# Product two of the last half of a down projection as a joint inner product, in a kernel that is bound by TensorE

## The chip, the cores and the metric

The kernel runs on one core of a Trainium2 chip. The metric is the device time of one execution in microseconds (us), taken as the median of several executions.

PE is TensorE's matmuls, PEld its weight loads, DVE is VectorE, ACT is ScalarE, SP (SyncE) the queue that issues most transfers. PSUM is the memory that matmuls write (this kernel declares eight banks of 512 float32 columns per partition), SBUF the working memory.

## The reference, cut to what matters

```python
# x: (1, 2048, 1024), bf16
xn = _layernorm(x, axis=-1)
s = _A_ref(xn, A_wqkv, A_wo)                       # linear attention
g = _silu(_B_ref(xn, B_w_gate, B_w_up, B_w_down))  # (silu(xn@wg) * (xn@wu)) @ wd
return x + s * g
```

The change concerns the last product, h @ wd. There h has 3584 columns, wd is 3584 x 1024.

## The kernel before

Large products are made with Winograd's form of Strassen's scheme: a product of 2 x 2 blocks takes seven block products rather than eight, at the price of sums of weight blocks and x blocks. "Product 2" (step 2 below) is one of those seven. The kernel cuts its token rows into two halves, `p`, and the output columns of the down projection into two halves, `h`. "The last half" is `(p, h) == (1, 1)`. In each half two sets (`w` = 0, 1) of 256 output columns, each two blocks of 128, run side by side.

For products 1 and 5 the two sets are joined: together they form a 2 x 2 block product again, and the scheme is applied a second time. That is the class `Joint`: seven inner products of 256 columns, in four parts a to d.

```python
class Set:
    def put1(self, a):                 # product 1 is in bank a: copy it to a second bank b
        self.a = a
        self.b = balloc()
        act([bank_r[a]], [bank_r[self.b]], ps[self.b][:, :], ps[a][:, :], ACT.Identity)
    def step(self, m):
        ...
        elif m == 2:
            self.grp(2, self.a, False)   # 14 matmuls of 512 columns, on top of product 1
            self.out(0, 0, self.a)
        elif m == 6:
            self.grp(6, self.b, False)
            self.c = balloc()
            tt(..., ps[self.c][:, :], ps[self.b][:, :], self.s5.ap(F32), ALU.add)
        ...
class Joint:
    def step(self, part):
        ...
        if part == 1:
            self.grp(6, y, 0)
            self.grp(2, x, 0)
            # the half-bank add: x's right half = y's left half + s
            tt([bank_r[y], s.r], [bank_r[x]], ps[x][:, 256:512], ps[y][:, 0:256], s.ap(F32), ALU.add)
        elif part == 2:
            self.grp(7, y, 0)            # writes y's left half: must wait for that add
            self.grp(3, x, 1)
            ...
ON_D  = "L 7_0 K0 6_1 7_1 K1 nj1a 3_0 nj1b 3_1 S nj1c 4a nj5a nj1d 4b nj5b n2_0 nj5c n2_1 nj5d n6_0"
END_D = "7_0 6_1 7_1 3_0 3_1 4_0 4_1"
```

Strings such as `END_D` are the order of steps: `n2_0` is product 2 of set 0 of the next half, `nj5b` part b of its joint product 5. A planner in the kernel then orders the instructions of every engine once, at build time, by estimated durations and deadlines. Each engine executes its list in order; only waits on semaphores remain.

## Time and profile before

| | before |
|---|---|
| median of the first 3 runs (range) | 712.78 us (711.15 to 713.37) |
| span of the profiled execution | 710.2 us |
| PE busy | 704.5 us, 4181 matmuls |
| DVE busy | 631.2 us |
| ACT busy | 424.9 us |

The span runs from the first to the last instruction on the core and is shorter than the time. Busy time counts overlapping neighbours once. The prediction below shows the lines.

### The profile page before, as it was taken

How to read it: one execution, taken by the hardware profiler on the slowest of the kernel's cores; microseconds unless marked ns; L12 is line 12 of the kernel's file. 1: busy time of each engine (PE TensorE's matmuls, PEld its weight loads, DVE VectorE, ACT ScalarE, POOL GpSimd, SP SyncE). 2: the span in 40 equal slices, each digit the busy share in tenths (PEclk: the TensorE clock that was granted, in tenths of full speed). 3: DMA queues.
4: the chain of work that ended last, by engine and by line, in shares of the span. 5: the costliest groups of instructions: out<-in, count | busy, mean ns of one | idle time of the engine just before them, and what ended most of it. 6: DMA issues, size and time to landing. Idle time of an engine off the chain costs nothing.

```text
span 710.2 us, 11444 instructions
## 1 busy us (share of the span) xinstructions
PE 704.5 (99%) x4181; PEld 388.1 (55%) x4181; DVE 631.2 (89%) x1534; ACT 424.9 (60%) x827; POOL 13.0 (2%) x34
## 2 busy tenths in 40 slices
PE   8999999999999999999999999999999999999997
PEld 3444445555555555556556455555555555565654
DVE  6999858989999999998958999999999999798863
ACT  5788766988679676664212257876886756531212
POOL 2111000000000000000000000000000000000000
PEclk9999999999999999999999999999999999999999
DMA  9654133346664253326498854322716241646763
GB/s 301 143 95 115 31 118 120 119 133 194 175 181 147 96 160 108 110 63 174 123 243 212 219 133 148 111 68 94 208 60 193 75 149 60 181 138 160 144 156 96
DMA packets 140871, 98.64 MB, mean 139 GB/s; under 512 B 34960, under 2 KB 137872, under 8 KB 140816
## 3 DMA queue, kind: packets, MB, share of 16 engines
q1 hardware_dynamic: 139472, 96.69, 49.1%
q10 hardware_dynamic: 1344, 1.25, 0.5%
q8 instruction: 32, 0.52, 0.3%
q14 instruction: 23, 0.19, 0.1%
HBM read 77.59 MB, written 12.71 MB: 127 GB/s over the span
## 4 chain that ended last, share of the span: by engine, by line
PE 98%; DMA 1%; SPq 0%; issue 0%; DVE 0%; ACT 0%
PE ps L309 98%; DMA H<-in_A_wqkv_dram 1%; PE ps L316 0%; DVE TM L453 0%; SPq L456 0%; SPq L760 0%; ACT TM L442 0%
## 5 line engine op out<-in xcount | busy, mean ns | idle before, releaser
L309 PE MATMUL ps<-X,W 128*128 128x512 f16 (+2 forms) x1348 | 282.6, 349 | 0.0
L442 ACT ACTIVATE TM<-ps 128x512 f16<-128x512 f32 (+3 forms) x386 | 202.7, 554 | 100.8 <-PE ps L309 97.3
L309 PE MATMUL ps<-H,W 128*128 128x512 f16 (+2 forms) x1096 | 218.6, 351 | 0.1
L309 PEld LDWEIGHTS ps<-X,W 128*128 128x128 f16 (+1 forms) x1348 | 130.0, 98 | 101.6 <-ACT H L442 1.0
L453 DVE TENSOR_TENSOR W<-W 128x256 f16<-128x256 f16 (+5 forms) x400 | 178.8, 479 | 2.7 <-PE ps L309 1.9
L309 PEld LDWEIGHTS ps<-H,W 128*128 128x128 f16 (+1 forms) x1096 | 105.9, 98 | 95.4 <-DVE ps L453 1.1
L453 DVE TENSOR_TENSOR ps<-ps,TM 128x256 f32<-128x256 f32 (+1 forms) x250 | 131.4, 527 | 14.8 <-PE ps L309 11.5
L442 ACT ACTIVATE ps<-ps 128x512 f32<-128x512 f32 (+1 forms) x174 | 85.7, 493 | 89.9 <-PE ps L309 89.4
L442 ACT ACTIVATE H<-ps 128x512 f16<-128x512 f32 (+1 forms) x132 | 78.5, 605 | 37.8 <-PE ps L309 37.8
L309 PE MATMUL ps<-P,W 128*128 128x256 f16 (+1 forms) x492 | 94.5, 318 | 0.0
L453 DVE TENSOR_TENSOR H<-H 128x1024 f16<-128x1024 f16 (+5 forms) x130 | 73.7, 581 | 0.7 <-ACT H L442 0.5
L442 ACT ACTIVATE TM<-TM 128x512 f16<-128x512 f32 (+1 forms) x70 | 44.0, 631 | 45.6 <-DVE TM L453 45.1
L309 PEld LDWEIGHTS ps<-P,W 128*128 128x128 f16 (+1 forms) x492 | 47.9, 98 | 27.0 <-ACT TM L442 0.8
L309 PE MATMUL ps<-W 128*128 128x256 f16 (+1 forms) x326 | 61.2, 282 | 0.0
L453 DVE TENSOR_TENSOR H<-H,TM 128x512 f16<-128x512 f16 (+1 forms) x120 | 48.0, 417 | 8.5 <-ACT H L442 8.3
L453 DVE TENSOR_TENSOR TM<-ps,TM 128x512 f32<-128x512 f32 (+3 forms) x63 | 41.6, 660 | 12.9 <-PE ps L309 12.0
L309 PEld LDWEIGHTS ps<-W 128*128 128x128 f16 (+1 forms) x326 | 31.1, 98 | 31.0 <-DVE ps L453 0.8
L309 PE MATMUL ps<-H,X 128*128 128x512 bf16 (+1 forms) x150 | 35.2, 379 | 0.4 <-DMA H<-in_A_wqkv_dram 0.4
L453 DVE TENSOR_TENSOR TM<-TM 128x512 bf16<-128x512 f16 (+2 forms) x73 | 29.2, 412 | 6.1 <-ACT TM L442 4.4
L309 PE MATMUL ps<-H,P 128*128 128x512 bf16 (+1 forms) x110 | 26.8, 379 | 0.0
L453 DVE TENSOR_TENSOR H<-ps,TM 128x512 f16<-128x512 f32 (+1 forms) x35 | 24.0, 686 | 2.2 <-PE ps L309 1.3
L453 DVE TENSOR_TENSOR TM<-TM,W 128x512 f16<-128x512 f16 (+1 forms) x39 | 14.1, 363 | 11.8 <-ACT TM L442 11.7
(111 smaller groups left out, 417.0 us busy)
## 6 DMA issues: line engine op xcount, KB each, us to landing
W<-in_B_w_up_dram SPq DMA_DIRECT2D x14, 1024.0 KB, 5.6
W<-in_B_w_gate_dram SPq DMA_DIRECT2D x13, 1024.0 KB, 5.3
W<-in_B_w_down_dram SPq DMA_DIRECT2D x14, 896.0 KB, 6.1
H<-r_scratch SPq DMA_DIRECT2D x32, 128.0 KB, 3.9
W<-m_scratch SPq DMA_DIRECT2D x4, 1024.0 KB, 5.4
s_scratch<-TM SPq DMA_DIRECT2D x32, 128.0 KB, 2.0
TM<-in_A_x_dram SPq DMA_DIRECT2D x16, 256.0 KB, 4.0
W<-in_A_x_dram SPq DMA_DIRECT2D x15, 256.0 KB, 3.4
```

Source lines behind the costliest of these rows:

```text
L309: last = h.matmul(o, l, r, start=st, stop=sp, skip_group_check=True)
L442: q = PL.op("act", reads, writes, lambda h: h.activation(o, i, func, **kw), nel(o) / (1000.0 if "bias" in kw or not isinstance(kw.get("sca ...
L453: return dve(reads, writes, lambda h: h.tensor_tensor(o, a, b, op), nel(o), 1.92 if fast else 0.96)
```

## The change

The intent: apply the second level of the scheme to product 2 as well, in the last half only. Product 1 can then no longer stay in the bank under product 2, so it is kept in SBUF and added afterwards. The x sums need space, and the R00 blocks of the hidden tensor are dead once product 1 of the last half is done. The core of the diff:

```diff
             def put1(self, a):
+                if self.two:
+                    self.b = a
+                    self.s1 = (self.s1r or s1_ring).take()
+                    act([bank_r[a]], [self.s1.r], self.s1.ap(F32), ps[a][:, :], ACT.Identity)
+                    return
+            def put2(self, x):
+                ...
+                d = (self.d2r or d2_ring).take()
+                tt([bank_r[x], self.s1.r], [d.r], d.ap(F32), ps[x][:, :], self.s1.ap(F32), ALU.add)
+                bfree(x)
+                self.evac(0, 0, d.ap(F32), d.r, None)
+        def tj_two():
+            B = {(k, j): hq("R10", k, j, 0, NU) for k in range(2) for j in range(2)}
+            t = {m: hq("R00", k, j, 0, NU) for m, (k, j) in TJ2.items()}
+            sub(t[7], B[1, 1], B[0, 1])
+            sub(t[5], B[0, 1], B[0, 0])
+            sub(t[6], B[1, 1], t[5])
+            sub(t[4], B[1, 0], t[6])
+                if (p, h) == (1, 1):
+                    self.joint["2"] = Joint(partial(self.jops, 2), lambda w, b: self.sets[w].put2(b))
+                    for s in self.sets:
+                        s.two = True
-        END_D = "7_0 6_1 7_1 3_0 3_1 4_0 4_1"
+        ON_E = "L 7_0 K0 6_1 7_1 K1 nj1a 3_0 nj1b 3_1 S nj1c 4a nj5a nj1d 4c nj5b 4d nj5c n6_0 nj5d"
+        END_D = "j2a 7_0 j2b 6_1 j2c 3_0 j2d 7_1 3_1 4_0 4_1"
```

Cut: facilities that this version leaves switched off (weight sums kept in DRAM, joint product 2 elsewhere), a cap on the planner's tuning passes, and moved buffers at the start of the second token half (the sums of one weight, the raw load of another).

More of the change, by code (lines that the diff above doesn't have):

```diff
@@ L130, in tune @@
         front = 0.0
-        while True:
+        for _ in range(90):
             prev, last, work, at = {}, {}, 0.0, None
@@ L584, in build_kernel, with __init__ @@
         class Set:
-            def __init__(self, ops, evac, dring):
-                self.ops, self.evac, self.dring, self.direct = ops, evac, dring, None
+            def __init__(self, ops, evac, dring, s1r=None, d2r=None):
+                self.ops, self.evac, self.dring, self.direct, self.two = ops, evac, dring, None, False
+                self.s1r, self.d2r = s1r, d2r
             def out(self, i, j, b):
@@ L612, in put1 @@
                 act([bank_r[a]], [bank_r[self.b]], ps[self.b][:, :], ps[a][:, :], ACT.Identity)
+            def put2(self, x):
+                if self.direct is not None:
+                    self.direct(0, 0, x, self.s1)
+                    bfree(x)
+                    return
+                d = (self.d2r or d2_ring).take()
+                tt([bank_r[x], self.s1.r], [d.r], d.ap(F32), ps[x][:, :], self.s1.ap(F32), ALU.add)
+                bfree(x)
+                self.evac(0, 0, d.ap(F32), d.r, None)
             def put5(self, e):
@@ L709, in build_kernel @@
         LINK = "7_0 nj1a 3_0 7_1 nj1b nj5a 3_1 nj1c nj5b 4_0 nj1d nj5c 4_1 n2_0 nj5d n6_0 n2_1 n6_1".split()
+        LINK3 = "7_0 nj1a 3_0 7_1 nj1b nj5a 3_1 nj1c nj5b 4_0 nj1d nj5c 4_1 nj2a nj5d n6_0 nj2b n6_1 nj2c".split()
         last_pair = [None]
@@ L722, in feed @@
             else:
-                for w in LINK:
+                for w in LINK3 if "2" in pair.joint else LINK:
                     if w[0] == "n":
@@ L727, in feed @@
                         prev.do(w)
+                    if w == "7_0" and prev is not None and prev.joint and "2" in prev.joint:
+                        prev.do("j2d")
             last_pair[0] = pair
@@ L1114, in strips, with wload @@
                     [hb(n, nm)[1].keys for n in range(8)])
-        def wload(src, joint, dt=BF16, rd=(), inh=(0, 0)):
+        w_scr = nc.dram_tensor("w_scratch", [18, 128, 4 * KB], FP16)
+        i_scr = nc.dram_tensor("i_scratch", [18, 2, 128, KB], FP16)
+        s1_ring, in2_ring, d2_ring = (Places([(a, o * KB) for a, o in at], 2 * KB) for at in (
+            [(H, 36)],
+            [(H, 36)],
+            [(H, 36)]))
+        TWO = []
+        NOSP = [('q', 1), ('g', 1), ('u', 1), ('g', 2), ('u', 2), ('g', 3), ('u', 3), ('g', 4), ('u', 4), ('g', 5), ('u', 5), ('g', 6), ('u', 6), ('q', 0), ('g', 0), ('u', 0), ('s', 0), ('s', 1)]
+        CH, IH, put = {}, {}, {}
+        def wload(src, joint, tag, dt=BF16, rd=(), inh=(0, 0)):
+            p, kind, n = tag
+            kept = {"g": 0, "u": 7, "s": 14, "q": 16}[kind] + n
             if inh[0]:
@@ L1128, in wload @@
             if inh[1]:
-                cs, keys = strips("T1", FP16)
+                cs, keys = strips((None, "T1", "T3")[inh[1]], FP16)
                 cv = cs.rearrange("p (m w) (kt n) -> p m w kt n", w=2, n=128)
                 cr = [Region(keys[2 * q] + keys[2 * q + 1]) for q in range(4)]
+                call, csem = cs, dsem("wch%d" % inh[1])
             else:
@@ L1135, in wload @@
                 cr = [c.sub(q * 2 * KB, 2 * KB).r for q in range(4)]
-            sums({(k, i): v[:, :, 4 * k:4 * k + 4, i * 128:i * 128 + 128] for k in range(2) for i in range(2)},
+                call, csem = c.ap(FP16), dsem("wc%s%d" % (c.a.name, c.off // KB))
+            cl = Region(sum((r.keys for r in cr), ()))
+            keep = (kind, n) not in NOSP
+            if p and keep:
+                kv = w_scr[kept]
+                dma([named("ws", kept)], [cl], call, kv.rearrange("p (b t) -> p b t", t=512) if inh[1] else kv, csem, 1024 * KB)
+            else:
+              sums({(k, i): v[:, :, 4 * k:4 * k + 4, i * 128:i * 128 + 128] for k in range(2) for i in range(2)},
                  [cv[:, q] for q in range(4)], [sr], cr)
+              if keep:
+                put.setdefault((kind, n), []).append((CH.get((kind, n), "j1a"), lambda: dma(
+                    [cl], [named("ws", kept)], w_scr[kept], call, dsem("wk%s%d" % (c.a.name, c.off // KB)), 1024 * KB,
+                    after=PL.lastpe)))
             def block(m):
@@ L1148, in wload @@
             inner = {}
-            for m in joint:
+            for m in joint + ((2,) if p and (kind, n) in TWO else ()):
                 bl, r = block(m)
-                t = in_ring.take()
+                t = (in2_ring if m == 2 else in_ring).take()
                 tv = t.ap(FP16).rearrange("p (m kt n) -> p m kt n", m=4, n=128)
@@ L1154, in wload @@
                 A = {(k, i): bl[:, i, 2 * k:2 * k + 2, :] for k in range(2) for i in range(2)}
-                sums(A, [tv[:, q] for q in range(4)], [r], tr)
+                place = "%s%d" % (t.a.name, t.off // KB)
+                held = named("wi", kept, m)
+                if p and m != 2 and keep:
+                    dma([held], [t.r], t.ap(FP16), i_scr[kept, m // 5], dsem("wi" + place), 256 * KB)
+                else:
+                    sums(A, [tv[:, q] for q in range(4)], [r], tr)
+                    if not p and keep:
+                        put.setdefault((kind, n), []).append((IH.get((kind, n), "j%da") % m, partial(
+                            dma, [t.r], [held], i_scr[kept, m // 5], t.ap(FP16), dsem("wj" + place), 256 * KB)))
                 inner[m] = (A, r, tv, tr)
@@ L1174, in build_kernel, with x_inner @@
         xin, qin = {}, {}
-        def x_inner(v, xin=xin, places=IN_AT):
-            for m, at in zip((1, 5), places):
+        def x_inner(v, xin=xin, places=IN_AT, ms=(1, 5)):
+            for m, at in zip(ms, places):
                 ap, r = v[XOF[m]]
@@ L1182, in x_inner, with joint_of @@
                 tt([r], [t[1][1]], t[1][0], B[1, 1], B[0, 1], ALU.subtract, True)
-                tt([r], [r], B[0, 1], B[0, 1], B[0, 0], ALU.subtract, True)
-                tt([r], [t[0][1]], t[0][0], B[1, 1], B[0, 1], ALU.subtract, True)
+                f, fr = t[3] if len(t) > 3 else (B[0, 1], r)
+                tt([r], [fr], f, B[0, 1], B[0, 0], ALU.subtract, True)
+                tt([r, fr], [t[0][1]], t[0][0], B[1, 1], f, ALU.subtract, True)
                 tt([r, t[0][1]], [t[2][1]], t[2][0], B[1, 0], t[0][0], ALU.subtract, True)
-                xin[m] = {1: (B[0, 0], r), 2: (B[1, 0], r), 3: (B[1, 1], r), 5: (B[0, 1], r), 6: t[0], 7: t[1], 4: t[2]}
-        def joint_of(jstat, s0, s1, xin=xin):
+                xin[m] = {1: (B[0, 0], r), 2: (B[1, 0], r), 3: (B[1, 1], r), 5: (f, fr), 6: t[0], 7: t[1], 4: t[2]}
+        def joint_of(jstat, s0, s1, xin=xin, two=False):
             def ops(m):
@@ L1194, in ops @@
                 return f
-            return {"1": Joint(ops(1), lambda w, b: (s0, s1)[w].put1(b)),
+            s0.two = s1.two = two
+            js = {"2": Joint(ops(2), lambda w, b: (s0, s1)[w].put2(b))} if two else {}
+            return {**js, "1": Joint(ops(1), lambda w, b: (s0, s1)[w].put1(b)),
                     "5": Joint(ops(5), lambda w, b: (s0, s1)[w].put5(b))}
@@ L1214, in q_load @@
         def q_load(p, s):
-            return wload(wqkv_v[:, :, s * 512:(s + 1) * 512], QJ[p][s])
+            return wload(wqkv_v[:, :, s * 512:(s + 1) * 512], QJ[p][s], (p, "q", s))
         def pq_tile(g, j):
@@ L1230, in q_pair @@
             s0, s1 = (xset(stat, w, XV[p], evac(w), d_ring) for w in range(2))
-            pair = Pair(s0, s1, joint_of(jstat, s0, s1) if QJ[p][s] else None, at)
+            pair = Pair(s0, s1, joint_of(jstat, s0, s1, two=p == 1 and ("q", s) in TWO) if QJ[p][s] else None, at)
             if go:
@@ L1287, in hb2, with gu_load @@
             return v, Region(hb(n, nm)[1].keys + hb(n + 1, nm)[1].keys)
-        def gu_load(k, n):
-            return wload((wg_v if k == "g" else wu_v)[:, :, n * 512:(n + 1) * 512], (1, 5), inh=(1, 1) if gate[0] and (k, n) == ("g", 0) else (0, 0))
+        def gu_load(p, k, n):
+            return wload((wg_v if k == "g" else wu_v)[:, :, n * 512:(n + 1) * 512], (1, 5), (p, k, n), inh={("g", 0): (1, 1), ("u", 0): (0, 2)}.get((k, n), (0, 0)) if p else (0, 0))
         sgs = {}
@@ L1309, in f @@
                     tt([orr, s.r], [orr], o, o, s.ap(FP16), ALU.mult, True)
-                    if w == 1 and (i, j) == (0, 0) and n in TJ_CUT:
-                        tj_first(p, TJ_CUT[n], n + 1)
+                    if w == 1 and (i, j) == (0, 0) and n in TJ_CUT[p]:
+                        tj_first(p, TJ_CUT[p][n], n + 1)
                     if w == 1 and (i, j) == (0, 1):
@@ L1321, in f @@
                     tt([orr, s.r], [orr], o, o, s.ap(FP16), ALU.mult, True)
+                    if w == 1 and (i, j) == (0, 0) and n in TJ_CUT[p]:
+                        tj_first(p, TJ_CUT[p][n], n + 1)
                 return f
@@ L1325, in gu_pair @@
                 s0.direct, s1.direct = direct(0), direct(1)
-            feed(Pair(s0, s1, joint_of(jstat, s0, s1), at))
+            feed(Pair(s0, s1, joint_of(jstat, s0, s1, two=p == 1 and (kind, n) in TWO), at))
         def h_sums(n):
@@ L1332, in h_sums, with s_load @@
             tt([v["R11"][1], v["T1"][1]], [v["T2"][1]], v["T2"][0], v["R11"][0], v["T1"][0], ALU.subtract, True)
-        def s_load(n):
-            return wload(m_v[:, :, n * 512:(n + 1) * 512], (1, 5), FP16, [named("mscr", n, g, k) for g in (0, 4) for k in range(4)])
+        def s_load(p, n):
+            return wload(m_v[:, :, n * 512:(n + 1) * 512], (1, 5), (p, "s", n), FP16, [named("mscr", n, g, k) for g in (0, 4) for k in range(4)])
         st_ring = Places([(TM, o * KB) for o in (20, 24, 21, 25)], KB)
@@ L1353, in build_kernel @@
         GB = 3584
-        TJ_CUT = {2: 0, 5: 3, 6: 6}
+        TJ_CUT = ({2: 0, 5: 3, 6: 6},) * 2
         NU = NPAIR // 2
@@ L1392, in tj_last @@
             sub(tq(TJ5[p][4], 0, NU), hq("T1", 1, 0, 0, NU), tq(TJ5[p][6], 0, NU))
+        TJ2 = {7: (0, 0), 5: (0, 1), 6: (1, 0), 4: (1, 1)}
+        def tj_two():
[5 more added lines that the diff above has]
+            sub(t[4], B[1, 0], t[6])
         def tj_view(p, m, k):
+            if m == 2:
+                if k in TJ2:
+                    return hq("R00", *TJ2[k], 0, NU)
+                return hq("R10", *{1: (0, 0), 2: (1, 0), 3: (1, 1)}[k], 0, NU)
             nm = "R00" if m == 1 else "T1"
@@ L1407, in build_kernel @@
         dd_ring = Ring(TM, 4 * KB, 2 * KB, 1)
+        de_ring = Places([(X, 14 * KB), (TM, 24 * KB)], 2 * KB)
+        dc_ring = Ring(W, 7 * KB, 2 * KB, 2)
         t4_rings = {(0, 0): Ring(X, 20 * KB, 2 * KB, 4), (0, 1): Ring(W, 7 * KB, 2 * KB, 3),
@@ L1422, in __init__ @@
                 self.t4 = []
-                self.sets = [Set(partial(self.ops, w), self.keep(w), dd_ring) for w in range(2)]
+                self.sets = [Set(partial(self.ops, w), self.keep(w), dd_ring, de_ring, dc_ring) for w in range(2)]
                 self.joint = {"1": Joint(partial(self.jops, 1), lambda w, b: self.sets[w].put1(b)),
                               "5": Joint(partial(self.jops, 5), lambda w, b: self.sets[w].put5(b))}
+                if (p, h) == (1, 1):
+                    self.joint["2"] = Joint(partial(self.jops, 2), lambda w, b: self.sets[w].put2(b))
+                    for s in self.sets:
+                        s.two = True
                 self.gv, self.xo, self.at = {}, {}, {}
@@ L1522, in do @@
                     self.joint[t[1]].step("abcd".index(t[2]))
+                    if "2" in self.joint and t == "j1d":
+                        tj_two()
+                    if "2" in self.joint and t == "j5d":
+                        self.prep(2)
                     if t == "j1c":
@@ L1528, in do @@
                         self.s67(1)
-                elif t in ("4a", "4b"):
-                    for n in (range(0, 8, 2) if t == "4a" else range(8, NPAIR, 2)):
+                elif t in ("4a", "4b", "4c", "4d"):
+                    for n in {"4a": range(0, 8, 2), "4b": range(8, NPAIR, 2), "4c": range(8, 12, 2), "4d": range(12, NPAIR, 2)}[t]:
                         for w in range(2):
@@ L1668, in down @@
             tj_second(p, 0, 6)
-            for seq, prev, nxt in ((IN_D, last_pair[0], d0), (ON_D, d0, d1), (END_D if p else OUT_D, d1, None)):
+            for seq, prev, nxt in ((IN_D, last_pair[0], d0), (ON_E if p else ON_D, d0, d1), (END_D if p else OUT_D, d1, None)):
                 if seq == END_D:
@@ L1692, in down @@
                         prev.do(t)
+                        if t == "7_0" and isinstance(prev, Pair) and "2" in prev.joint:
+                            prev.do("j2d")
             last_pair[0] = nxt
@@ L1705, in pump @@
                 k, p, s = lq.popleft()
-                got[k, p, s] = q_load(p, s) if k == "q" else s_load(s) if k == "s" else gu_load(k, s)
+                got[k, p, s] = q_load(p, s) if k == "q" else s_load(p, s) if k == "s" else gu_load(p, k, s)
         pump(2)
@@ L1728, in turn_pass @@
             gate[0] = 1
-            raw_ring.__init__([(X, 0), (W, 0 * KB), (X, 0), (W, 8 * KB), (W, 16 * KB)] + [(W, 0), (W, 8 * KB), (W, 16 * KB)] * 5, 8 * KB)
-            cmb_ring.__init__([(X, 8 * KB), (X, 8 * KB)] + [(W, 24 * KB), (W, 32 * KB)] * 8, 8 * KB)
+            raw_ring.__init__([(X, 0), (W, 0 * KB), (X, 8 * KB), (W, 8 * KB), (W, 16 * KB)] + [(W, 0), (W, 8 * KB), (W, 16 * KB)] * 5, 8 * KB)
+            cmb_ring.__init__([(X, 8 * KB)] + [(W, 24 * KB), (W, 32 * KB)] * 8, 8 * KB)
             in_ring.__init__([(W, 14 * KB), (TM, 8 * KB), (W, 24 * KB), (W, 26 * KB), (W, 42 * KB), (W, 44 * KB)]
@@ L1744, in build_kernel @@
                 if p == 0 and (k, n) in (("g", 0), ("u", 0), ("q", 1)):
-                    at = {"6_1": [build_m]}
+                    at["6_1"] = [build_m]
                     if k == "u":
                         at["6_0"] = [build_m]
+                for w, fn in put.pop((k, n), ()):
+                    at.setdefault(w, []).append(fn)
                 if (p, k, n) == (0, "g", 1):
@@ L1752, in build_kernel @@
                 if (k, n) == ("u", 1):
-                    at = {"j1d": [partial(recip, p)]}
+                    at.update({"j1d": [partial(recip, p)]})
                 if (k, n) == ("g", 2):
-                    at = {"j1a": [partial(normalise_part, p, 0, 0)], "2_1": [partial(normalise_part, p, 0, 1)]}
+                    for w, fn in (("j1a", partial(normalise_part, p, 0, 0)), ("2_1", partial(normalise_part, p, 0, 1))):
+                        at.setdefault(w, []).insert(0, fn)
                 if (k, n) == ("u", 2):
-                    at = {"j1a": [partial(normalise_part, p, 1, 0)], "2_1": [partial(normalise_part, p, 1, 1)], "4_1": [partial(combos, QV)]}
+                    for w, fn in (("j1a", partial(normalise_part, p, 1, 0)), ("2_1", partial(normalise_part, p, 1, 1)), ("4_1", partial(combos, QV))):
+                        at.setdefault(w, []).insert(0, fn)
                 if (k, n) == ("g", 3):
-                    at = {"2_1": [partial(x_inner, QV, qin, QIN_AT)]}
+                    at.setdefault("2_1", []).append(partial(x_inner, QV, qin, QIN_AT))
+                if p == 1 and (k, n) in TWO and "2_1" in at:
+                    at["6_1"] = at.pop("2_1")
                 if last_pair[0] is not None and (p, k, n) == (1, "q", 0):
@@ L1762, in build_kernel @@
                 elif k == "q":
+                    if (p, n) == (1, 1) and TWO:
+                        x_inner(XV[1], places=(((X, 1536), (X, 2560), (X, 5 * KB), (X, 6 * KB)),), ms=(2,))
                     q_pair(p, n, st, at)
```

## The prediction

> **What bounds the kernel now.** I read the page first: part 1 for the engines, part 2 for the clock, part 4 for the chain that ended last.
>
> ```profile
> PE 704.5 (99%) x4181; PEld 388.1 (55%) x4181; DVE 631.2 (89%) x1534; ACT 424.9 (60%) x827; POOL 13.0 (2%) x34
> ...
> PEclk9999999999999999999999999999999999999999
> ...
> PE 98%; DMA 1%; SPq 0%; issue 0%; DVE 0%; ACT 0%
> ```
>
> TensorE is never idle after the start, its clock is full, and 98% of the chain is matmuls. So the time is the number of matmul columns, plus a start and a tail. A busy share alone does not prove that, so I went to the timeline of TensorE in the last half of the down projection, the stage that the change edits. The columns are start, duration, engine and line, operation, tiles, count:
>
> ```profile
> 666.88 1.69 PE L309 MATMUL ps<-H,W 128*128 128x256 f16 x14
> 668.41 1.36 PE L309 MATMUL ps<-X,W 128*128 128x256 f16 x9
> ...
> 681.63 18.29 PE L309 MATMUL ps<-H,W 128*128 128x512 f16 x84
> 699.76 0.38 PE L309 MATMUL ps<-X,W 128*128 128x512 f16 x1
> ```
>
> Read start to start, not by duration (a matmul is recorded as 273 or 379 ns because neighbours overlap). 84 wide ones take 699.76 - 681.63 = 18.13 us, **215.8 ns each**. 14 narrow ones take 668.41 - 666.88 = 1.53 us, **109.3 ns each**. These are the prices for everything below. The windows view shows what else has room there (busy us and count per engine):
>
> ```profile
> 643.50:663.40 19.90, 19.87 (x114) 10.94 (x113) 14.51 (x30) 3.71 (x7) 0.00 (x0) 1.00 0.97 202
> 663.40:699.50 36.10, 36.10 (x197) 19.07 (x196) 23.87 (x47) 7.48 (x15) 0.00 (x0) 1.00 0.46 113
> ```
>
> In these 56.0 us VectorE (third column pair) is busy 38.4 us, ScalarE 11.2 us.
>
> **What the Trainium skill says.** (1) "TensorE: Matmul & The Clock Gate", section Back-to-back issue gap, gives N/2.4 + 2.5 ns between matmuls of N columns: 215.8 and 109.2 ns for 512 and 256. The trace agrees to 0.1 ns. The same section's sustained 131 ns at 512 columns does not fit this trace. (2) "Perfetto Trace Analysis", section Identifying the Most-Contended Engine, warns that matmul busy share is a poor measure of the roofline and prefers the weight-load share. Here weight loads are 55% while there is no headroom, so the start-to-start spacing decides. (3) "VectorE: DVE Perf Modes", section The perf-mode tier table, has tensor_tensor at twice the rate for 16-bit data in SBUF and at single rate with a PSUM operand. The groups of VectorE in this stage agree:
>
> ```profile
> L453 DVE TENSOR_TENSOR X<-H 128x1024 f16<-128x1024 f16 x13 | 8.5, 683 | 0.0
> L453 DVE TENSOR_TENSOR W<-W 128x896 f16<-128x896 f16 x11 | 6.6, 618 | 0.3 <-PE ps L309 0.2
> L453 DVE TENSOR_TENSOR TM<-ps,TM 128x512 f32<-128x512 f32 x4 | 2.8, 690 | 5.5 <-PE ps L309 5.5
> L453 DVE TENSOR_TENSOR ps<-ps,TM 128x256 f32<-128x256 f32 x4 | 1.7, 428 | 2.3 <-PE ps L309 2.3
> ```
>
> **The change part by part.** Product two of the last half was 2 sets x 14 = 28 matmuls of 512 columns. It becomes the seven inner products of the joint scheme, 7 matmuls each: 49 of 256 columns. Counting both built programs gives exactly that: 2469 to 2441 wide, 1386 to 1435 narrow, nothing else of TensorE altered.
> - **TensorE**: removed 28 x 215.8 = 6.04 us; added 49 x 109.3 = 5.36 us; net **-0.69 us**. The formal saving of one eighth (0.76 us) loses 0.07 us to the fixed cost of 21 more matmuls. A weight load takes 98 ns (groups of the page), below the 109 ns spacing, so it stays hidden.
> - **VectorE**: four x sums of 7x256 = 1792 elements into the R00 blocks. From 618 ns at 896 and 683 ns at 1024 elements, the slope is 0.51 ns, so about 1073 ns each: 4.3 us. Four weight sums at 620 ns: 2.5 us. Two half-bank adds at 428 ns: 0.9 us. Two adds of product two to the kept product one at 690 ns: 1.4 us. Together +9.0 us, beside TensorE. 38.4 + 9.0 = 47.4 of 56.0 us, so it fits on average.
> - **ScalarE**: two half-bank copies (about 0.37 us each), and the copies of product one go to SBUF rather than PSUM (597 against 582 ns). Under 1 us more, with 45 us free.
> - **Moved**: product two now stands between products 7, 6 and 3 rather than before product 6. That takes away cover. In the built program before, between the inner product two of joint five (which frees the sum blocks for overwriting) and product 6 of set 0 there are 8.3 us of matmuls; after the change only 4 wide and 14 narrow, 0.86 + 1.53 = 2.4 us. In that time VectorE must wait for the matmuls to retire (about 0.2 us), do two 896-element sums (1.24 us) and one half-bank add (0.43 us): 1.9 us. So a margin of 0.5 us. Walking the VectorE order on from there with these durations, the sums for product 7 come 3 us early, for product 6 of set 1 nearly 3 us early. No stall by the walk, but the first margin is thin.
> - **The tail** is the one place off TensorE. Its end before:
>
> ```profile
> 706.41 0.28 ACT L442 ACTIVATE TM<-ps 128x128 f16<-128x128 f32 x1 [0.61 <-PE ps L309]
> ...
> 706.72 0.23 DVE L453 TENSOR_TENSOR TM<-TM 128x128 f16<-128x128 f16 x1 [0.33 <-ACT TM L442]
> 706.86 0.22 DVE L453 TENSOR_TENSOR TM<-ps,TM 128x128 bf16<-128x128 f16 x1
> 707.27 0.23 DVE L453 TENSOR_TENSOR TM<-ps,TM 128x128 bf16<-128x128 f16 x1 [0.19 <-PE ps L316]
> 707.53 0.36 ACTq L1586 DMA_DIRECT2D out_dram<-TM  x1
> ```
>
> The last multiply waits only for ScalarE (the bracket). In the built program after the change, two VectorE adds stand ahead of it: the one that before came just after it, and a 512-element add of a transposed block, which before was already done. 0.22 + 0.42 us starting near 706.5 end near 707.1 instead of 706.72, so everything after starts about **0.3 us later**. That block's 256 KB store also becomes the last one issued by the sync queue, about half a microsecond later than before; such stores land in 3.3 us by the page. I book **+0.4 us** (0.3 to 0.6).
> - **Rest of the diff**: the lists that would keep weight sums in DRAM, or use joint product two elsewhere, are switched off (every weight is excluded, the other list is empty), so no transfer is added; the counts confirm it. The cap of 90 tuning passes does not bind: a build with a counter makes 22 passes before, 23 after. At the start of the second token half one weight's sums move to H and one raw load to another part of X. TensorE lost nothing measurable there, so nothing can be won.
>
> Sum: -0.69 + 0.4 = **-0.3 us**.
>
> **The rivals.** (a) *Clean gain*: the tail is hidden after all, -0.7 us, near 711.9. For: the new adds are short. Against: VectorE is in order. (b) *VectorE becomes the bound* between joint five and product 3: the margin of 0.5 us is eaten by the 9.0 us of added work, TensorE waits 0.5 to 2 us, giving 712.8 to 714.3. For: before, VectorE has stretches of 5.00 busy in 5.00 us in this stage, just where the x sums go. Against: elsewhere the kernel runs VectorE at 39.9 of 40 us without TensorE losing time. (c) *The tail eats all*: the late store ends last and costs 0.7 us or more, time as before, 712.6. (d) *The second half's start stalls* on the moved buffers, +0.5 to 1 us. Against: their sums can start earlier than before, not later.
>
> **Range and chances.** The three runs before spread over 711.15 to 713.37, their median is 712.78 and the profiled one took 711.96; the mean of the four is 712.3. I take 712.6 as base, between both, and subtract 0.3: **712.3 us**. The scatter of runs (about 1 us) is larger than the effect, so the range is mostly scatter, with more room above for (b): 711.1 to 713.6. Two per cent is 14 us; nothing here reaches a tenth of that. Faster 0.01, same 0.98, slower 0.01.
>
> **What would show each step.** Right: the page has 4202 matmuls; wide and narrow spacings stay 216 and 109 ns; from the first joint-five matmuls to the last 128-column ones TensorE has no gap; its last matmul starts about 0.7 us earlier than 706.2; from there to the end of the span takes 0.3 to 0.6 us longer. VectorE's busy time rises by about 9 us, four groups H<-H of about 1.07 us among it. Wrong: a weight load just before product 6 of set 0 or a joint part that waited for VectorE for over 0.3 us (rival b); a last matmul no earlier than before with no such gap (the prices are wrong); a gap of TensorE near 400 us (rival d). A change over 2 us either way would mean that something outside this list decides.

## The result, and the profile after

In the first rounds the median went from 712.45 us (6 runs, 711.15 to 713.37) to **712.05 us** (6 runs, 711.76 to 712.17). The ratio is 0.9995 with a 95% interval of 0.9982 to 1.0008: the same. (A ratio is the mean time of one kernel's runs over the mean of the other's from the same rounds, so it is not quite the ratio of the medians.) The medians do not establish which kernel is faster; the traces do, for everything but the start.

The page after, parts 1 and 4 (engines, then the chain that ended last):

```profile
PE 703.2 (99%) x4202; PEld 389.9 (55%) x4202; DVE 638.5 (90%) x1546; ACT 425.9 (60%) x829; POOL 12.9 (2%) x34
...
PE 96%; DMA 3%; DVE 1%; SPq 0%; ACTq 0%; issue 0%
```

There are 21 more matmuls, as counted, and 12 more instructions on VectorE. The kernel is bound as before. (The 3% of DMA in the chain are two transfers, one at the start and one late weight load ahead of 191 us, which a later experiment takes up.)

**Where the gain shows.** I mark two places that both kernels share: *the entry*, the wide matmul after a fixed gap of 0.19 us in the down projection of the second token half, and *product 4*, the start of product 4 of set 0 in the last half. (The view merges 32 matmuls there: 14 wide ones of set 0, then 14 narrow and 4 of 128 columns of set 1; an expectation below calls them all wide.) First the timeline of TensorE before, then after (start, duration):

```profile
643.73 3.63 PE L309 MATMUL ps<-H,W 128*128 128x512 f16 x16
699.76 4.94 PE L309 MATMUL ps<-X,W 128*128 128x512 f16 x32
```

```profile
643.73 3.63 PE L309 MATMUL ps<-H,W 128*128 128x512 f16 x16
699.44 4.94 PE L309 MATMUL ps<-X,W 128*128 128x512 f16 x32
```

From the entry to product 4 takes 699.76 - 643.73 = 56.03 us before and 55.71 us after: 0.32 us less, where 0.69 us were expected.

**Where the other 0.37 us are.** The chain view after, in order of time (start, duration, what):

```profile
643.73 28.88 PE ps L309 x171
672.61 0.02 issue
672.64 0.62 DVE W L453
673.26 0.35 DVE ps L453
673.61 0.05 issue
673.66 30.72 PE ps L309 x186
```

The chain leaves TensorE for about a microsecond: it passes through a weight sum on VectorE (`W`, 0.62 us), then the half-bank add (`ps`), then TensorE again. The timeline confirms a wait there:

```profile
672.87 0.59 PE L309 MATMUL ps<-X,P 128*128 128x512 f16 x2
673.66 0.94 PE L309 MATMUL ps<-P,W 128*128 128x256 f16 x7 [0.20 <-DVE ps L453]
```

Two wide matmuls from 672.87 would let the next start at 672.87 + 2 x 0.216 = 673.30; it starts at 673.66, so 0.36 us are lost. (The bracket says 0.20 us because the recorded end of the last matmul lies late.) The group that waits is part c of joint product 5.

**The tail.** ScalarE's and VectorE's last instructions after, which answer to the last lines in the prediction:

```profile
706.17 0.28 ACT L442 ACTIVATE TM<-ps 128x128 f16<-128x128 f32 x1 [0.69 <-PE ps L309]
706.20 0.55 DVE L453 TENSOR_TENSOR TM<-TM 128x512 bf16<-128x512 f16 x2
...
706.81 0.23 PE L316 MATMUL ps<-ident,TM 128*128 128x128 f16 x1 [0.67 <-DVE TM L453]
706.91 0.46 SPq L456 DMA_DIRECT2D out_dram<-TM  x1
...
707.33 0.37 ACTq L1666 DMA_DIRECT2D out_dram<-TM  x1
```

From product 4 to the last store's issue took 707.53 - 699.76 = 7.77 us before, 707.33 - 699.44 = 7.89 us after: 0.12 us more. Net in the trace: -0.32 + 0.12 = **-0.20 us**, which is also the difference of the spans (710.0 against 710.2), because both traces happen to reach the entry at 643.73 us.

### The profile page after: what moved, and what is told of

Read it like the earlier page. It is cut to its first block, busy times and chain, and to the rows that moved or that the text cites. A ratio compares the mean times of both kernels' runs of the same rounds, so it can differ in the third digit from the quotient of the medians.

```text
span 710.0 us, 11504 instructions
## 1 busy us (share of the span) xinstructions
PE 703.2 (99%) x4202; PEld 389.9 (55%) x4202; DVE 638.5 (90%) x1546; ACT 425.9 (60%) x829; POOL 12.9 (2%) x34
## 4 chain that ended last, share of the span: by engine, by line
PE 96%; DMA 3%; DVE 1%; SPq 0%; ACTq 0%; issue 0%
PE ps L309 96%; DMA W<-in_B_w_up_dram 1%; DMA H<-in_A_wqkv_dram 1%; DVE W L453 0%; SPq L456 0%; PE ps L316 0%; DVE ps L453 0%; DVE TM L453 0%; ACTq L456 0%; ACTq L779 0%
## 5 line engine op out<-in xcount | busy, mean ns | idle before, releaser
L453 DVE TENSOR_TENSOR W<-W 128x256 f16<-128x256 f16 (+5 forms) x404 | 181.1, 482 | 1.9 <-PE ps L309 0.7
L309 PEld LDWEIGHTS ps<-H,W 128*128 128x128 f16 (+1 forms) x1117 | 108.0, 98 | 92.6 <-DVE ps L453 1.1
L442 ACT ACTIVATE ps<-ps 128x512 f32<-128x512 f32 (+2 forms) x173 | 84.9, 492 | 89.9 <-PE ps L309 89.4
L453 DVE TENSOR_TENSOR H<-H 128x1024 f16<-128x1024 f16 (+6 forms) x134 | 78.0, 597 | 0.6 <-ACT H L442 0.4
L309 PEld LDWEIGHTS ps<-H,X 128*128 128x128 f16 (+1 forms) x150 | 14.4, 98 | 17.0 <-ACT X L442 0.7
```

What stands on the lines that cost most here:

```text
L309: last = h.matmul(o, l, r, start=st, stop=sp, skip_group_check=True)
L442: q = PL.op("act", reads, writes, lambda h: h.activation(o, i, func, **kw), nel(o) / (1000.0 if "bias" in kw or not isinstance(kw.get("sca ...
L453: return dve(reads, writes, lambda h: h.tensor_tensor(o, a, b, op), nel(o), 1.92 if fast else 0.96)
```

## The experiments

All outputs are right. The main reading is the piece from the entry to product 4, because nothing in it depends on when the program's first transfers land. Some expectations counted it from the down projection of the *first* token half instead, from the last narrow matmul ahead of the same gap (349.58 us in both traces); that gives 350.18 us before and 349.86 us after, the same difference.

| kernel | entry | product 4 | piece | product 4 to last store's issue | span |
|---|---|---|---|---|---|
| before | 643.73 | 699.76 | 56.03 | 7.77 | 710.2 |
| before, again | 643.19 | 699.22 | 56.03 | 7.77 | 709.7 |
| rest of the diff only | 643.65 | 699.69 | 56.04 | 7.76 | 710.2 |
| changed | 643.73 | 699.44 | 55.71 | 7.89 | 710.0 |
| changed, again | 642.88 | 698.59 | 55.71 | 7.88 | 709.2 |
| add first | 643.36 | 698.70 | 55.34 | 7.88 | 709.3 |
| add first, timed | 644.33 | 699.67 | 55.34 | 7.88 | 710.2 |
| tail's multiply with priority | 644.02 | 699.74 | 55.72 | 7.88 | 710.3 |
| both of these (slow transfer) | 643.51 | 699.08 | 55.57 | 7.88 | 709.7 |
| add first, both tail edits | 645.18 | 700.52 | 55.34 | 7.77 | 711.3 |
| add first, transpose put back | 643.61 | 698.95 | 55.34 | 7.97 | 709.5 |
| x sums twice (slow transfer) | 643.25 | 699.96 | 56.71 | 7.77 | 710.8 |
| x sums thrice | 644.37 | 700.14 | 55.77 | 7.88 | 710.7 |

The entry itself moves by 2.3 us from run to run (642.88 to 645.18). The piece repeats to 0.01 us wherever a kernel that differs only outside it was run again, with one exception ("both of these", explained there).

### The add ahead of the weight sum

```diff
-                    tt([bank_r[y], s.r], [bank_r[x]], ps[x][:, 256:512], ps[y][:, 0:256], s.ap(F32), ALU.add)
+                    tt(...same...).urgent = self.hurry     # 4.0 for joint 5 of the last half, else 0
```

> One edit on the changed kernel: the half-bank add of joint five's second step is scheduled ahead of the first weight sum for product 6 (both wait for the same matmuls). Theory (the 0.36 us gap of TensorE near 673 us comes from that add standing second in VectorE's order, so joint five's third step waits 0.62 us too long): the gap closes to under 0.1 us and TensorE's 32 wide X,W matmuls of product 4 start near 699.1 us, against 699.44 in the changed kernel and 699.76 before, 0.69 us ahead of before as the matmul prices say. Rival (VectorE is simply full there, any order loses): the gap moves to product 6 of set 0, which then waits 0.2 to 0.4 us, and product 4 still starts near 699.4.

The timeline of VectorE and TensorE around the place, in this kernel:

```profile
672.26 0.43 DVE L453 TENSOR_TENSOR ps<-ps,TM 128x256 f32<-128x256 f32 x1
672.49 0.59 PE L309 MATMUL ps<-X,P 128*128 128x512 f16 x2
672.60 1.27 DVE L453 TENSOR_TENSOR W<-W 128x896 f16<-128x896 f16 x2
...
672.92 0.93 PE L309 MATMUL ps<-P,W 128*128 128x256 f16 x7
```

The add now stands ahead of the two sums, and part c follows the wide matmuls after 672.92 - 672.49 = 0.43 us, that is 2 x 0.216 with no gap. Product 6 shows no gap either. The piece is 55.34 us: **0.69 us less than before the change**, the full price difference of the matmuls. Product 4 starts at 698.70 rather than 699.1 because this run's entry was 0.37 us earlier; the piece corrects for that. The theory holds, and its rival (VectorE full, any order loses) falls.

### The tail's multiply with priority

```diff
-                    tt([gh.r, sh.r], [gh.r], gh.ap(FP16), gh.ap(FP16), sh.ap(FP16), ALU.mult, True)
+                    tt(...same...).urgent = 8.0 * (h > 0)
```

> One edit on the changed kernel: the last multiplies of the finish get priority, so that on VectorE the last 128-column multiply stands right after the add of the block before it and not also behind the 512-element add. PE gap near 673 stays as in the changed kernel, product 4 starts near 699.44. Theory (the misplaced add delays the tail): time from the start of product 4 to the last store's issue on ScalarE's queue shrinks from 7.89 us (707.33 - 699.44) to about 7.77, as before the change (707.53 - 699.76 = 7.77), so the saving is 0.1 us, not the 0.3 to 0.4 that was predicted; but the adds of the 512 block and the 256 KB store now come after. Rival (the late 256 KB store ends the run): the span from product 4 to the end gets longer than 10.6 us.

A failed experiment: the piece was 55.72 us and the tail 7.88 us, as in the changed kernel. Reading the built program again showed that VectorE's last seven instructions stand in the same order as without the edit. The planner takes the 512-element add when it is ready and the multiply is not, unless the multiply's deadline is over 10 us nearer. It tests nothing.

### Both of these, timed

> Both edits together, the version meant to beat both kernels. Theory: product 4 starts near 699.1 us, the last store is issued near 706.9, the span is about 709.5 against 710.0 (changed) and 710.2 (before), the median 0.7 us below that of before, that is a ratio near 0.9990, hardly clear of the scatter. Rival: gap or tail return in another place and the span is 709.9 to 710.2.

With the tail edit void, this is nearly the version with the add first. The median was 712.26 us (5 runs, 711.16 to 713.18) against 711.95 us before (9 runs), ratio 1.0003 (0.9990 to 1.0017). Product 4 at 699.08 us, as expected, is luck: the entry came 0.22 us early. The one trace was disturbed, and instructively so: the piece took 699.08 - 643.51 = 55.57 us, with a gap of 0.21 us left before part c although the add came first. The chain shows why:

```profile
656.16 8.46 DMA TM<-TM
...
664.64 0.43 DVE TM L453
...
672.36 0.54 DVE W L453
672.90 0.35 DVE ps L453
```

A transposing transfer (`TM<-TM`) took 8.46 us. The median of the 30 in this trace is 3.2 us, but this one, issued 12.65 us after the entry, is a long one in all kernels with this order: 5.48 us in the changed kernel, 8.21 us in "add first, timed". VectorE, in order, waited 0.83 us for it, and 8 us later its list was still late. In "add first, timed", with the same order on VectorE up to 681 us, it waited 0.58 us and no gap followed. So this VectorE list absorbed 0.58 us, and of 0.83 us it passed 0.21 us on to TensorE.

### The rest of the diff alone

```diff
-                if (p, h) == (1, 1):
-                    self.joint["2"] = ...
-                    for s in self.sets:
-                        s.two = True
-        END_D = "j2a 7_0 j2b 6_1 j2c 3_0 j2d 7_1 3_1 4_0 4_1"
+        END_D = "7_0 6_1 7_1 3_0 3_1 4_0 4_1"      # and ON_D in place of ON_E
```

> The changed kernel with the joint product two undone: old sequences, no kept product one, no x sums, but all other edits of the diff (moved buffers at the start of the second token half, switched-off lists, cap on tuning) in place. Theory (the rest of the diff does nothing): TensorE's records as before, 4181 matmuls, product 4 starts within 0.1 us of 699.76, the median within 0.5 us of that of before. Rival (the moved buffers win or lose something that hid the effect): product 4 starts 0.3 us or more away from 699.76, with the difference arising between 350 and 450 us.

4181 matmuls, a piece of 56.04 us, a tail of 7.76 us, and 349.50 to 643.65 us between the two down projections against 349.58 to 643.73 before: 294.15 us in both. The ratio was 1.0002 (0.9990 to 1.0015). The moved buffers and the lists that are switched off neither win nor lose.

### The changed kernel and the one with the add first, in the same rounds

> The changed kernel unaltered, timed in the same rounds as the version with the add first, so that they can be compared. Theory: median 711.7 to 712.3; in the trace the gap of 0.36 us before joint five's third step and, from the gap of 0.19 us at the entry of the down projection's first half (349.58 us) to the start of product 4 in the last half, 349.86 us again, against 350.18 before: this piece has no jitter of the start in it. Rival: the gap was an accident of that one profile, then it is gone or elsewhere here.

> The version with the half-bank add first, timed. In its look the piece from the first half's entry to product 4 took 349.49 us: 0.37 us less than in the changed kernel and 0.69 less than before. Theory: the same piece again within 0.05 us unless a slow transfer delays VectorE; median 0.3 to 0.4 us below that of the changed kernel in the same rounds and 0.6 us below before, a ratio of about 0.999. Rival (runs scatter by more than this because of transfers, and the gain is not measurable in medians): medians within 0.3 us of each other in either order.

The pieces came again: 55.71 and 55.34 us. The medians were 712.10 us (5 runs) for the changed kernel, 711.62 us (6 runs) with the add first, 711.73 us (11 runs) before; ratios 1.0001 (0.9989 to 1.0014) and 0.9998 (0.9985 to 1.0012). Before now looks faster than changed, where the first rounds said the opposite. With the add first the median was 0.48 us below the changed kernel, but 0.11 us below before where 0.6 us were expected. The rival of the latter expectation stands in substance (though 0.48 us is more than its 0.3): runs of one kernel lie up to 2.3 us apart in these rounds (711.0 to 713.3 for the kernel before), and 0.2 or 0.6 us is not to be had from five of them.

### The kernel before once more

> The kernel before, unaltered, for a second trace of it. Theory (the scatter of the medians is the start and the transfers of the first half, which the change does not touch): the matmul position at the first half's entry differs from 349.58 us by 0.3 us or more, while the piece from there to product 4 is 350.18 us again within 0.05. Rival: the piece itself varies by 0.3 us, then the changed kernel's 349.86 means nothing.

The same place in the first token half's down projection was reached at 349.04 us rather than 349.58, and the piece from there to product 4 was 350.18 us again (from the entry 56.03 us again). A gap near 191 us, which my changed trace had (0.30 us) and my first trace of before had not, is in this trace as well (0.20 us ahead of 190.49), and it is missing in "changed, again". In the changed trace it waits for sums that follow a late weight load. It is no part of the change: the planned order of all engines is the same in both kernels up to the loads of the second token half.

### The add first, and the tail truly reordered

```diff
-                        if turns and n == (4 if h == 2 else 10):
+                        if turns and n == (99 if h == 2 else 10):   # transpose after the last matmuls
-                    tt([o.r, q.r], [q.r], ..., ALU.add, True)
+                    a = tt([o.r, q.r], [q.r], ..., ALU.add, True)
+                    if (p, self.h, w, i, j) == (1, 1, 1, 0, 1):
+                        a.urgent = -30.0                            # the 512-element add last
```

> The add first, and the tail changed for real this time (the earlier edit of the tail left VectorE's last seven instructions in the same order, so it tested nothing): the transpose of the second-to-last block stands after the last two matmuls, as before the change, and the last multiply stands ahead of the 512-element add. Theory (the 0.12 us that the tail grew by are this transpose, 0.08 us, and the add, 0.05 us): from the start of product 4 to the issue of the last store on ScalarE's queue 7.77 us instead of 7.88, the span the same or shorter. Rival (the 256 KB store ends the run): it is now issued last on the sync queue, after 707 us, and the span minus the start of product 4 grows from 10.6 us to 10.8 us or more.

The tail came out as the theory had it, the end of the run as its rival had it. The tail to the last store's issue on ScalarE's queue is 7.77 us again, but the run ended later after product 4: 711.3 - 700.5 = 10.8 us rather than 10.6. The timeline of the stores:

```profile
708.07 0.37 SPq L456 DMA_DIRECT2D out_dram<-TM  x1
708.29 0.37 ACTq L1667 DMA_DIRECT2D out_dram<-TM  x1
```

The 256 KB store (first line) was issued 708.07 - 700.52 = 7.55 us after product 4, against 706.91 - 699.44 = 7.47 us in the changed kernel; in the kernel before it was 706.57 - 699.76 = 6.81 us. The trace has their landings too: here the large store landed last, at 710.78 us, 0.17 us after the small one; in the changed kernel it landed at 709.35 us, 0.20 us ahead of the small one. In "x sums twice" the planner chose this order of the tail by itself (7.77 us in the table), and there too the large store landed last and the run ended 10.8 us after product 4. So the tail has two ends: the last small store and this large one, and freeing one delays the other. (The run as a whole was late from its start; its entry is the latest of all.)

### The add first, only the transpose put back

The first of the two tail edits alone.

> The add first, and of the tail only the transpose of the second-to-last block put back behind the last two matmuls; the order on VectorE and of the stores stays as in the changed kernel. Meant as the version that beats both. Theory: the piece from the first half's entry to product 4 takes 349.49 us (before 350.18, changed 349.86); from product 4 to ScalarE's last store issue 7.80 us (before 7.77, changed 7.89); the span after product 4 10.5 us (before 10.5, changed 10.6, the version with both tail edits 10.8 because its 256 KB store came last). Median 0.5 us below the changed kernel if the start's jitter averages out, else within 0.5 us of it either way. Rival: the tail grows again because the 256 KB store comes later, span after product 4 of 10.8 us.

The piece is 55.34 us once more. The tail is 7.97 us, not 7.80: the last matmul starts 6.39 us after product 4, as before the change (6.47 us in the changed kernel), but then VectorE's order bites:

```profile
705.59 0.28 ACT L442 ACTIVATE TM<-ps 128x128 f16<-128x128 f32 x1 [0.61 <-PE ps L309]
705.65 0.23 DVE L453 TENSOR_TENSOR TM<-ps,TM 128x128 bf16<-128x128 f16 x1 [0.21 <-PE ps L316]
705.79 0.55 DVE L453 TENSOR_TENSOR TM<-TM 128x512 bf16<-128x512 f16 x2
706.40 0.23 PE L316 MATMUL ps<-ident,TM 128*128 128x128 f16 x1 [0.79 <-DVE TM L453]
```

From ScalarE's last activation to the last transpose: 0.81 us here, 0.64 us in the changed kernel, 0.59 us before. The multiply (the second of the `x2`) stands behind the 512-element add. The span after product 4 is 10.59 us by the trace's full digits, as in the changed kernel (10.59). The median was **711.38 us** (5 runs, 710.99 to 712.62) against 712.42 us before (9 runs), ratio 0.9991 (0.9977 to 1.0006). That is the lowest median of the timed kernels and in the direction of the traces, but not clear of the scatter.

### The x sums made twice and three times

```diff
                     if "2" in self.joint and t == "j1d":
-                        tj_two()
+                        for _ in range(2):       # or 3
+                            tj_two()
```

> The four x sums of joint product two are made twice (the same values, written again), 4.3 us more VectorE work in the stage; the scheduler reorders around it. Theory (VectorE's work beside the matmuls costs nothing while it fits: 47.4 + 4.3 = 51.7 of 56.0 us): product 4 starts within 0.4 us of 699.44, counted from the first half's entry. Rival (VectorE is already the bound in this stage): TensorE waits grow by 2 us or more and product 4 starts after 701.5.

> The x sums made three times: 8.7 us of VectorE work more than the changed kernel, 17.6 us of the 17.6 us that were idle in the stage before. Made twice, TensorE lost 0.99 us more than in the changed kernel. Theory (VectorE becomes the bound once its idle time is used up where the work must be done, in about 664 to 674 us): the piece takes 352 to 356 us, 2 to 6 us more than the changed kernel. Rival (there is room yet, the 0.99 us was one unlucky order): under 351.2 us.

Twice: the piece grew to 56.71 us, 1.00 us over the changed kernel. Thrice: 55.77 us, only 0.06 us over it, although VectorE ran fuller. The windows view of the kernel with three times (VectorE is the third pair):

```profile
643.50:663.40 19.90, 19.87 (x114) 10.89 (x113) 19.02 (x32) 3.71 (x7) 0.00 (x0) 1.00 0.95 216
663.40:699.50 36.10, 35.84 (x223) 21.48 (x222) 34.76 (x65) 8.23 (x17) 0.00 (x0) 1.00 0.47 117
```

VectorE is busy 53.8 of 56.0 us here, and TensorE's piece is hardly longer. In the kernel with two, part c waits again. Its chain has the first line, its timeline the others:

```profile
656.75 7.87 DMA TM<-TM
...
670.67 3.34 DVE L453 TENSOR_TENSOR H<-H 128x1792 f16<-128x1792 f16 x3
...
673.93 0.62 DVE L453 TENSOR_TENSOR W<-W 128x896 f16<-128x896 f16 x1
674.46 0.42 DVE L453 TENSOR_TENSOR ps<-ps,TM 128x256 f32<-128x256 f32 x1
...
674.94 0.94 PE L309 MATMUL ps<-P,W 128*128 128x256 f16 x7 [0.76 <-DVE ps L453]
```

Three x sums in a row, 3.34 us, then a weight sum, then the half-bank add that part c needs. But this trace was disturbed as well: VectorE waited 1.08 us for the slow transfer (the first line), and its chain runs from there to that add without another wait. So how much of the 0.92 us that TensorE lost before part c is order and how much is the transfer is not shown.

TensorE lost another 0.42 us ahead of 673.24. In both kernels the planner put seven narrow matmuls (`H,W`) ahead of part c, and by the trace they waited for an activation of ScalarE. In the kernel with three they lost 0.42 us as well, and that is nearly all of its loss against the add-first kernel (55.77 against 55.34 us); its part c follows without a gap.

The expectation for twice missed on both sides: 0.99 us by its count, against at most 0.4 (theory) or at least 2 (rival). For thrice the theory that VectorE becomes the bound was wrong and its rival held: 350.56 us by its count, with 0.62 us of that lost near 408 us, outside the stage.

## Why the prediction was right or wrong

The time, 712.3 us predicted and 712.05 us measured, and "same" were right. The net of -0.3 us was near the -0.20 us of the traces, but that is luck: two of its terms were off and cancelled.

1. **Bound and prices: right.** TensorE's columns set the time. The -0.69 us for the matmuls is exact: it is what remained (56.03 - 55.34 us) once the gap was removed.
2. **"No stall by the walk, but the first margin is thin": the step that failed.** I walked VectorE's list only to product 6, with 2.4 us of cover. Part c of joint product 5 comes first, with four wide matmuls, 0.86 us, as cover; it needs the half-bank add, and that stood behind a weight sum of 0.62 us which nothing needed yet. It cost 0.36 us; putting the add first, with the same work, removed it. This is rival (b) in place and mechanism (VectorE gates joint five; its sign, a joint part that waits over 0.3 us, came true), below its lower size of 0.5 us, but not its reason: VectorE is not the bound there, since with 8.7 us more of its work the piece grew by 0.06 us and no gap before part c was left.
3. **The tail: mechanism right, size off.** I booked +0.4 us; it measured +0.12 us. Of this 0.08 us is the second-to-last block's transpose, which the planner put ahead of the last two matmuls (6.39 to 6.47 us from product 4 to the last matmul) and which I had counted on neither side; the add ahead of the last multiply cost 0.05 us (0.59 to 0.64 us), not 0.3. Because of that early transpose the 512-element add could start at 706.20 rather than after 706.5. With the transpose put back, the add costs 0.22 us, nearer to what I had said. The late 256 KB store (rival c) did not end the run in the changed kernel; with both tail edits it landed last, and the span after product 4 grew.
4. **VectorE's additions: right.** An x sum took 1082 ns (predicted 1073), the first line; the second is for the end of this point:

```profile
L453 DVE TENSOR_TENSOR H<-H 128x1792 f16<-128x1792 f16 x4 | 4.2, 1082 | 0.0
...
L453 DVE TENSOR_TENSOR TM<-ps,TM 128x512 bf16<-128x512 f16 x1 | 0.4, 418 | 0.0
```

   With four weight sums, two half-bank adds (427 ns) and two final adds (685 ns) the recorded durations add up to 9.0 us, as predicted. VectorE's busy time rose by only 7.3 us. Busy time counts overlapping neighbours once, and a fuller list has more of them: from 640 us on the durations in the two traces add up to 50.0 and 59.0 us, the busy time to 45.0 and 52.5 us. One reading in the prediction's point (3) was too wide: the groups shown agree with a single rate for a PSUM operand, but they are float32. With a 16-bit PSUM operand the same operation took 418 ns at 512 elements (the second line), as with both operands in SBUF (417 ns), against 690 ns in float32. No term of the sum rests on this.
5. **Rival (d) and the rest of the diff: right.** The kernel with the rest alone has before's piece and before's time between the down projections.
6. **The scatter: right in size, without a cause.** It arises ahead of the stage that the change edits: the entry moves by 2.3 us between the traces, the piece of one kernel by 0.01 us. Most of it is the start: at a short gap of TensorE near 165 us that all traces share, they already lie 1.9 us apart (165.05 to 166.97 us).

What stays open: which order of the tail is best for both of its ends, and how much of the loss with the x sums twice is order.

## What to carry to other kernels

When an engine is full and in order, ask of each short instruction that gates the bottleneck what stands directly ahead of it in its list, and how much cover the bottleneck has until it is needed; the busy share does not answer that. When a change is worth less than the scatter, measure between two marks inside the trace that both kernels share: here that repeated to 0.01 us, but for one trace with a slow transfer, where medians of five runs changed sign. Removing work that served as cover, even cheap work, has to be priced with the waits that it covered.

## What the Trainium skill lacked or had wrong

- "TensorE: Matmul & The Clock Gate", section Back-to-back issue gap: the sustained 131 ns per matmul of 512 columns is not met; this stream of weight load and matmul pairs runs at 215.8 ns, as the page's "isolated" formula says (and 109.3 ns at 256 columns).
- "Perfetto Trace Analysis", section Identifying the Most-Contended Engine: of the two measures that it names for TensorE, MFU (the share of the peak rate of arithmetic) and weight-load share, the second is not a measure of headroom in such a stream. It was 55% with TensorE without a gap over tens of microseconds. MFU was not worked out here.
- "VectorE: DVE Perf Modes", section The perf-mode tier table: its single rate for tensor_tensor with any PSUM operand holds here for float32 alone (690 ns at 512 elements). With a 16-bit PSUM operand it took 415 to 418 ns in the 13 traces, one such operation in each, as fast as from SBUF; the text below that table allows it, the table does not.
- No page that I read told how far one transposing transfer can stray: the one issued 12.65 us after the entry took 5.5 to 8.5 us from run to run, against a median of 3.2 us in a run, and at 8.46 us it left VectorE's list late 8 us after it landed.
